# Feature projections on two 64-row array tiles, batch 1 loaded ahead of the MoE weights, and a planner that models shared DMA rings

## The chip, the cores and the metric

The kernel runs on one core of one Trainium2 chip. The metric is the device time of one execution in microseconds, as the median of several runs. A profile of one run gives the "span", the time from its first to its last instruction. The time is about 2 us longer than the span.

## The reference, cut to what matters

Two layers follow each other: a linear attention with random features (8 batches, 8 heads, 576 positions, 64 dimensions, 128 features), and an MLP ("MoE" in the code) on its output.

```
def phi(x):                      # x: q or k, scaled
    proj = einsum('bhsd,md->bhsm', x, omega)      # contraction over only d = 64
    h = proj - sum(x * x) / 2
    return exp(h - max(h)) / sqrt(m)
kv  = einsum('bhsm,bhsd->bhmd', phi(k), v);  z = sum_s phi(k)
out = einsum('bhsm,bhmd->bhsd', phi(q), kv) / (phi(q) . z + 1e-6)
x   = out as (4608, 512)
h   = x @ w_in                   # 512 -> 2048
y   = (h * sigmoid(1.702 h)) @ w_out              # 2048 -> 512
```

The two MLP products take 1152 matmuls of 512 columns. At the 0.216 us per matmul that the trace shows (0.86 us for four) that is 249 us, three quarters of the time.

## The kernel before

The program is planned when it is built. Every operation is put into a graph with an estimated cost and a priority, a small simulation decides the order on each engine, and the engines then run that order with semaphores.

Attention works in 32 steps: 8 batches of 4 head pairs. Q and K of a step lie transposed in a tile TT with 128 rows: 64 rows are the dimensions of one position, the other 64 those of its neighbour. Omega stands twice in a block-diagonal matrix omB, so that one matmul over 128 rows projects both positions; half of what it multiplies is zero.

```python
        for hd, t0, c0, o in (("a", 2, 0, 1280), ("b", 6, 4, 1792)):       # K: two banks
            gr = bank()
            g.add(PE,
                [mm(at(gr, 0, 256), Tb(t0), omB[:, :]), mm(at(gr, 256, 512), Tb(t0 + 1), omB[:, :])],
                240, key, reads=[("Tk", tt)] + OM, grp=gr)
            reduce(0, 4, c0, gr)                                            # DVE: max
            exp(gr, 512, o, ["k" + hd], key + 200)                          # ACT
        gr = bank()                                                         # tail: last 64 positions
        g.add(PE, [mm(at(gr, 128, 256), TLo, om_o), mm(at(gr, 0, 128), om_e, TLo)], 115, key + K_L, ...)
        ...
        for nm, w_, o in (("q0", om_e, 0), ("q1", om_o, 512)):              # Q: two banks
            gr = bank()
            g.add(PE, mm(at(gr, 0, 512), w_, Tq), 216, key + K_Q, ...)
            exp(gr, 512, o, [nm], key + K_Q + 100)
```

From batch 2 on, Q and K are transposed by DMA (into TT), and so is the attention's output (from OO into XT, the input of the MLP), all on the queue of SP. The heads of Q and K for the next batches are loaded by POOL's queue. At the start the loads go in this order: batch 0, half of batch 1's Q and K, w_in, the other half, w_out.

The softmax here doesn't subtract the row's maximum and nothing guards it: scores larger than these inputs give would overflow.

## Time and profile before

| | before |
|---|---|
| time, median | 329.97 us |
| span of the profiled run | 328.3 us, granted clock 0.995 |
| PE busy | 311.3 us, 95% |
| DVE, ACT, POOL busy | 58%, 60%, 26% |

These lines are from the page of the kernel before: the busy time of each engine, the busy share of PE and the granted clock in 40 slices of the span (9 is 90% or more), and the chain of work that ended last.

```profile
PE 311.3 (95%) x2091; PEld 163.2 (50%) x2129; DVE 189.5 (58%) x420; ACT 197.1 (60%) x396; POOL 86.6 (26%) x176
...
PE   2697999999999999999999999999999999999995
...
PEclk9989999999999999999999999999999999999999
...
PE 88%; DVE 5%; DMA 2%; issue 1%; SPq 1%; POOL 0%; ACT 0%; POOLq 0%
```

PE is busy 90% or more everywhere but in the first four slices and the last. A PE that is busy isn't yet at its peak, so the price of the projections is read from start to start. The next lines are PE's timeline of the kernel before in a late step (start in us, length in us, engine, line, operation, output and inputs, rows and columns, shape, count). A length contains about 0.16 us of pipeline that the next matmul overlaps. A few matmul records are missing from a trace, so a group of four can show as three.

```profile
233.33 0.22 PE L363 MATMUL PB<-omB,TL 128*128 128x128 bf16 x1
233.39 0.22 PE L363 MATMUL PB<-TL,omB 128*128 128x128 bf16 x1
233.44 0.38 PE L363 MATMUL PB<-TT,omB 128*128 128x512 bf16 x1
233.66 1.03 PE L363 MATMUL HT<-XT,WIN 128*128 128x512 bf16 x4
...
235.39 0.38 PE L363 MATMUL PB<-TT,omB 128*128 128x512 bf16 x1
235.60 1.03 PE L363 MATMUL HT<-XT,WIN 128*128 128x512 bf16 x4
...
237.64 0.60 PE L363 MATMUL PB<-omB,TT 128*128 128x256 bf16 x4
238.08 1.03 PE L363 MATMUL HT<-XT,WIN 128*128 128x512 bf16 x3
```

Tail 0.11 us (233.33 to 233.44), one half of Q 0.22 us, the other 0.21, K 0.44 us (237.64 to 238.08): 0.98 us per step.

The third view gives busy times by stretch for the kernel before; the columns are length, then busy us (count) of PE, PEld, DVE, ACT and POOL, then granted clock, DMA share and GB/s.

```profile
0.00:60.00 60.00, 48.72 (x432) 29.61 (x438) 39.33 (x102) 40.41 (x87) 30.83 (x60) 0.97 1.09 182
...
140.00:180.00 40.00, 39.69 (x289) 21.32 (x293) 26.86 (x64) 27.07 (x57) 14.89 (x30) 1.00 0.99 180
180.00:200.00 20.00, 19.89 (x131) 10.28 (x132) 13.40 (x28) 13.67 (x29) 3.04 (x8) 1.00 0.92 177
```

PE has some 11 us without work in the first 60 us and 0.1 to 0.2 us in each 20 us later.

### The profile page before, as it was taken

Reading aid. Unit: us, or ns where it says so; the run is one execution under the profiler, and the core shown is the slowest. Engines: PE = TensorE matmul, PEld = TensorE weight load, DVE = VectorE, ACT = ScalarE, POOL = GpSimd, SP = SyncE. Lnnn points to the kernel's source line nnn. Section 1 sums busy time; section 2 is a strip of 40 time slices with the busy share of each in tenths; the row PEclk is TensorE's granted clock in tenths of the full one; section 3 lists DMA queues with packets and bytes.
Section 4 is the critical chain, followed back from the end, with each engine's and each line's share of the span. In section 5 each row is a group of like instructions: output and inputs, shape, how many; then the busy total and the mean of one; then the engine's idle time right before and its main releaser. Section 6 shows DMA issues by size and latency. Waiting matters only on the chain.

```text
span 328.3 us, 5569 instructions
## 1 busy us (share of the span) xinstructions
PE 311.3 (95%) x2091; PEld 163.2 (50%) x2129; DVE 189.5 (58%) x420; ACT 197.1 (60%) x396; POOL 86.6 (26%) x176
## 2 busy tenths in 40 slices
PE   2697999999999999999999999999999999999995
PEld 1474655455555555555555555555544444444442
DVE  3397975458538786677468667675565434434300
ACT  2879664567738868777566657665663434344411
POOL 8398043043425226233316022222220000000000
PEclk9989999999999999999999999999999999999999
DMA  7999989989999999969979973311121011000033
GB/s 114 215 229 206 224 143 129 290 159 213 216 190 200 241 160 183 234 150 163 279 142 174 268 100 87 84 53 54 52 54 52 32 48 50 32 34 32 32 90 73
DMA packets 92939, 44.97 MB, mean 137 GB/s; under 512 B 59632, under 2 KB 88304, under 8 KB 92912
## 3 DMA queue, kind: packets, MB, share of 16 engines
q1 hardware_dynamic: 71760, 32.03, 44.3%
q0 software_dynamic: 21152, 12.59, 27.6%
q8 instruction: 17, 0.28, 0.4%
q14 instruction: 10, 0.08, 0.1%
HBM read 36.73 MB, written 9.44 MB: 141 GB/s over the span
## 4 chain that ended last, share of the span: by engine, by line
PE 88%; DVE 5%; DMA 2%; issue 1%; SPq 1%; POOL 0%; ACT 0%; POOLq 0%
PE OB L363 37%; PE HT L363 37%; PE PB L363 8%; PE SB L363 5%; DMA VS<-in_v_dram 2%; DVE NM L592 2%; DVE OO L733 1%; SPq L425 1%; DVE GT L792 1%; DVE TT L499 1%; PE SB L746 0%; SPq L447 0%; DVE RD L725 0%; POOL VP L652 0%; PE OB L534 0%
## 5 line engine op out<-in xcount | busy, mean ns | idle before, releaser
L792 DVE SCALAR_TENSOR_TENSOR GT<-TH,HT 128x512 bf16<-128x512 f32 x144 | 98.3, 685 | 75.6 <-ACT TH L787 75.1
L363 PE MATMUL HT<-XT,WIN 128*128 128x512 bf16 x555 | 139.6, 379 | 2.1 <-ACT WW L636 0.8
L363 PE MATMUL OB<-WOUT,GT 128*128 128x512 bf16 x559 | 137.8, 379 | 0.9
L787 ACT ACTIVATE TH<-HT 128x512 f32<-128x512 f32 x144 | 85.9, 597 | 73.8 <-PE HT L363 70.9
L603 ACT ACTIVATE QKP<-PB 128x512 bf16<-128x512 f32 (+1 forms) x143 | 77.8, 556 | 25.4 <-DVE NM L592 19.3
L363 PEld LDWEIGHTS OB<-WOUT,GT 128*128 128x128 bf16 x576 | 55.4, 98 | 59.9
L363 PEld LDWEIGHTS HT<-XT,WIN 128*128 128x128 bf16 x576 | 54.7, 98 | 58.4 <-ACT XT L498 0.9
L592 DVE TENSOR_REDUCE NM<-PB 128x4 f32<-128x512 f32 (+1 forms) x89 | 48.8, 564 | 26.1 <-PE PB L363 25.9
L641 POOL TENSOR_TENSOR WW<-WW,mask 128x2 f32<-128x2 f32 x32 | 6.3, 196 | 145.4 <-ACT WW L636 145.4
L652 POOL TENSOR_TENSOR VP<-VS,WW 128x512 bf16<-128x512 f32 x32 | 33.5, 1048 | 2.2 <-DMA VS<-in_v_dram 2.2
L821 ACT ACTIVATE OS<-OB 128x512 f32<-128x512 f32 x36 | 21.5, 597 | 20.6 <-PE OB L363 20.5
L733 DVE TENSOR_TENSOR OO<-SB,RD 128x320 bf16<-128x320 f32 x61 | 27.2, 478 | 0.1
L363 PE MATMUL PB<-omB,TT 128*128 128x256 bf16 x124 | 22.3, 282 | 1.7 <-ACT QKP L603 0.9
L363 PE MATMUL PB<-TT,omB 128*128 128x512 bf16 x54 | 19.7, 379 | 0.0
L363 PEld LDWEIGHTS SB<-KVZ,QKP 128*128 128x128 bf16 x305 | 14.0, 98 | 6.7 <-issue 0.2
L363 PEld LDWEIGHTS SB<-VP,QKP 128*128 128x128 bf16 x279 | 12.9, 99 | 8.1 <-POOL VP L662 2.3
L363 PE MATMUL SB<-VP,QKP 128*128 128x65 bf16 (+1 forms) x279 | 14.8, 198 | 2.0 <-POOL VP L662 1.8
L410 POOL DMA_DIRECT2D QK<-in_k_dram x17 | 13.4, 791 | 11.4 <-DMA TT<-QK 7.5
L363 PEld LDWEIGHTS PB<-omB,TT 128*128 128x128 bf16 x124 | 11.1, 100 | 8.6 <-ACT QKP L603 1.6
L363 PE MATMUL SB<-KVZ,QKP 128*128 128x65 bf16 x305 | 15.1, 195 | 0.0
L499 DVE CAST KVZ<-SB 128x130 bf16<-128x130 f32 x30 | 8.7, 289 | 11.0 <-PE SB L363 10.7
L410 POOL DMA_DIRECT2D QK<-in_q_dram x17 | 13.0, 766 | 0.0
(68 smaller groups left out, 134.0 us busy)
## 6 DMA issues: line engine op xcount, KB each, us to landing
out_dram<-OS SPq DMA_DIRECT2D x32, 256.0 KB, 2.5
VS<-in_v_dram SPq DMA_DIRECT2D x12, 512.0 KB, 8.8
QK<-in_k_dram POOLq DMA_DIRECT2D x15, 256.0 KB, 7.2
QK<-in_q_dram POOLq DMA_DIRECT2D x15, 256.0 KB, 8.9
VS<-in_v_dram SPq DMA_DIRECT2D x8, 256.0 KB, 8.4
WIN<-in_moe_w_in_dram POOLq DMA_DIRECT2D x4, 512.0 KB, 10.1
WOUT<-in_moe_w_out_dram POOLq DMA_DIRECT2D x4, 512.0 KB, 17.4
QLF<-in_q_dram SPq DMA_DIRECT2D x16, 64.0 KB, 4.4
```

Of the source, the lines that this page charges most:

```text
L363: return lambda e: e.matmul(o() if callable(o) else o, lhsT=l, rhs=r, **kw)
L410: POOL, lambda e, dst=dst, so=so: e.dma_start(dst, so), 800, key,
L425: SP, lambda e, dst=dst, so=so: e.dma_start(dst, so), 120, key,
L499: fv = lambda e: e.tensor_copy(out=o, in_=src())
L592: lambda e: e.tensor_reduce(out=NM[vs][:, c0 : c0 + w], in_=bass.AP(TILE[gr.bank], i, [[512, 128], [128, w], [1, 128]]), axis=AX.X, op=ALU ...
L603: lambda e: e.activation(out=X[:, o : o + w], in_=at(gr, 0, w)(), func=ACTF.Exp, scale=scale),
L641: lambda e: e.tensor_tensor(out=WW[vs][:, 0:2], in0=bass.AP(WW[vs], 10, [[12, 128], [0, 2]]), in1=mask2[:, :], op=ALU.mult,),
L652: lambda e: e.tensor_tensor(out=VP[vs][:, 2:10, 0:64], in0=bass.AP(V, vo + 64, [[vrow, 128], [64, 8], [1, 64]]), in1=bass.AP(WW[vs], 2, [[ ...
L733: lambda e, gr=gr, x=x: e.tensor_tensor(out=OO[os_][:, 5 * x : 5 * x + 5, :], in0=bass.AP(TILE[gr.bank], 0, [[512, 128], [65, 5], [1, 64]] ...
L787: lambda e, gr=gr, th=th: e.activation(out=TH[th][:, :], in_=at(gr, 0, 512)(), func=ACTF.Tanh, scale=0.851),
L792: lambda e, gr=gr, th=th, jc=jc: e.scalar_tensor_tensor(out=GT[gi][:, jc, :], in0=TH[th][:, :], scalar=1.0, in1=at(gr, 0, 512)(), op0=ALU. ...
L821: lambda e, gr=gr, os_=os_: e.activation(out=OS[os_][:, :], in_=at(gr, 0, 512)(), func=ACTF.Copy, scale=0.5),
```

## The change

The intent: a contraction over 64 rows needs only half of the array, so two such products can run side by side on two tiles of 64 rows. From batch 2 on, the K projections of even and odd positions run as pairs, and so do those of Q, K and Q in one visit of PE that fills four PSUM banks (JOIN). The tail is projected once per batch for all four steps. Batches 0 and 1 stay on full rows. Batch 1's Q and K are all loaded before w_in. V of batches 2 to 7 moves from SP's queue to POOL's (V_SW). The planner gets costs for the visits (PEC, in ns) and a model in which the DMA queues share the rings; all priorities were searched anew.

```diff
+PE_T = (0, 1)
+JOIN = True
+V_SW = 2
+PEC = dict(K=325.0, Q=315.0, KQ=540.0, L=345.0)
 ...
+        rt = b not in PE_T
+        lo = (slice(0, 64), slice(64, 128)) if rt else (slice(0, 128), slice(0, 128))
+        OMR = [omB[lo[par], 128 * par : 128 * par + 128] for par in range(2)]
+        def project(cols, cost, kk, reads):
+            gs = [bank() for _ in cols]
+            ems = [[mm(at(gr, o, o + w), l, r) for o, w, l, r in c] for gr, c in zip(gs, cols)]
+            if rt:
+                em = [f for j in range(0, len(ems), 2) for fs in zip_longest(*ems[j : j + 2]) for f in fs if f is not None]
+                g.add(PE, em, PEC[cost], kk, reads=reads + OM, grp=gs)
 ...
+        if rt and JOIN:
+            gr = project(kcols + qcols, "KQ", key, [("Tk", tt), ("Tq", tt)])
 ... (DMA queues in the planner: a queue's rate falls when the other is active)
-    load_qk(1, 0, 4, P["LD"] + -10, "a", after=[("k", 0, 0)])
-    for c in range(4):
-        load_win(c, P["LD"] + -5 + c, after=gate)
-    load_qk(1, 4, 4, P["LD"] + 0, "b", after=gate)
+    for c in range(4):
+        load_win(c, P["Lw"] + c, after=gate)               # Lw = 769
+    load_qk(1, 0, 4, P["Lb"], "a", after=gate)             # Lb = -19112: first
+    load_qk(1, 4, 4, P["Lb"] + 2, "b", after=gate)
```

## The prediction

> **What bounds the kernel.** By the table of the page PE is busy 311.3 us (95%) of a 328.3 us span; DVE 58%, ACT 60%, POOL 26%. The busy-by-stretch view shows PE full from 40 us on (39.68 of each 40 us) until the last matmul at 324 us; then one eviction and one store. The chain of waits is 88% PE. The exception is the start: PE was busy 3.7, 7.8, 7.85 and 9.5 us in the first four stretches of 10 us (11 us idle). There DMA is saturated (0.84 to 1.27 of 16 engines), and from 20 to 30 us DVE and ACT are busy 9.2 of 10 us. First MoE matmul: 29.9 us.
>
> **What the change saves.** In the PE timeline a steady attention step spends, start to start, 0.43 us on four 128x256 K projections, 0.43 on two 128x512 Q projections and 0.11 on the tail pair: 0.97 us. Half of the rows of each projection are zeros. From batch 2 on the change puts even and odd columns on two 64-row tiles side by side: half the columns, 0.43 us for K and Q together, and the tail once per batch. The Trainium skill, "TensorEngine Tiling (Array Packing)", Key Properties, says that tiles run in parallel but that changing the tiling mode drains the engine. This trace has no mode change; a matmul lasts 379 ns at a spacing of 216, so a drain can expose up to 0.16 us. The new planner's constants are 540 ns for the joint visit and 345 for the tail, about 110 ns over the half-length stream; I take these as estimates. Per step: 0.54 + 0.345/4 = 0.63 us instead of 0.97, saving 0.345; times 24 steps = 8.3 us, all on the critical path because PE is the limit there. With free switches it would be about 11 us; with 0.16 us in and out, about 4.
>
> Batches 0 and 1 stay on full rows: no change. POOL, DVE and ACT get slightly less work, off the path.
>
> **What it adds.** A joint visit opens all four P/S banks at once, so PE, in order, must find all four evacuated; a step has about 8 us and needs about 2.4 us of exps. I allow 1 us of new small PE waits. V loads of batches 2 to 7 move to POOL's queue: no cost expected.
>
> **The start.** W_in now comes behind all of batch 1's Q and K (1.2 MB newly ahead of it: about 5 us at that stretch's 220 GB/s). So the first MoE matmul moves to about 33 us, with batch 1's attention further along. ACT and DVE are nearly full there, so little PE work can be pulled forward; better planning should give back a bit. I book -2 us, doubt 3 us either way.
>
> **Sum.** 329.8 - 8.3 + 1 - 2 = 320.5; I shade to 319.5 us. Range 314 to 325. Faster by over 2% (below 323.2): 0.79; same: 0.19; slower: 0.02.
>
> **What would show it.** Projections per step near 0.55 us in the PE timeline from batch 2 on, pairs of 64-row matmuls starting within a few ns; PE still full (under 0.3 us idle per 20 us) from 40 us; a batch period of about 33.0 us instead of 34.3; first MoE matmul at 32 to 35 us; PE idle of the first 40 us within 3 us of the old 11.
>
> **What would make it wrong.** Drains of over 0.3 us per visit; tiles that don't overlap; PE waits for exps before joint visits; weights so late that PE starves between 30 and 60 us; loads of later batches late because PE now outruns the DMA (still 93% busy from 160 to 200 us).

## The result, and the profile after

| | before | after |
|---|---|---|
| time, median of 4 runs | 329.97 us (329.63 to 330.24) | 325.63 us (325.16 to 326.83) |
| ratio | | 0.9873, 95% interval 0.9851 to 0.9895 |
| span of the profiled run | 328.3 us | 323.0 us |
| PE busy | 311.3 us | 305.2 us |

A ratio is the mean time of one kernel's fast runs over that of the other's of the same rounds, so it isn't quite the ratio of the medians. The change gained 1.3%, not the 3.1% of the prediction, and the time lies 0.6 us above the stated range. From the page of the new kernel, busy times and chain:

```profile
PE 305.2 (94%) x2194; PEld 152.3 (47%) x2233; DVE 191.9 (59%) x394; ACT 194.2 (60%) x389; POOL 91.1 (28%) x149
...
PE 84%; DMA 9%; ACT 3%; POOL 2%; issue 1%; DVE 0%; POOLq 0%
```

DMA has 9% of the chain, where it had 2%. (The chain counts the whole length of a transfer that it passes through, not only the time that PE waited for it.) Next, PE's timeline of the new kernel around a tail visit, and then around a joint visit.

```profile
64.52 1.03 PE L412 MATMUL HT<-XT,WIN 128*128 128x512 bf16 x4
65.48 0.39 PE L412 MATMUL SB<-TL,omB 64*128 64x512 bf16 x1
65.48 0.39 PE L412 MATMUL PB<-omB,TL 64*128 64x128 bf16 x4
65.81 0.39 PE L412 MATMUL OB<-WOUT,GT 128*128 128x512 bf16 x1
```

```profile
66.68 1.03 PE L412 MATMUL HT<-XT,WIN 128*128 128x512 bf16 x4
67.64 0.23 PE L412 MATMUL SB<-omB,TT 64*128 64x128 bf16 x1
67.64 0.23 PE L412 MATMUL PB<-omB,TT 64*128 64x128 bf16 x1
...
67.82 0.22 PE L412 MATMUL SB<-omB,TT 64*128 64x128 bf16 x1
67.82 0.22 PE L412 MATMUL PB<-omB,TT 64*128 64x128 bf16 x1
67.87 0.38 PE L412 MATMUL SB<-TT,omB 64*128 64x512 bf16 x1
67.88 0.38 PE L412 MATMUL PB<-TT,omB 64*128 64x512 bf16 x1
68.18 1.04 PE L412 MATMUL OB<-WOUT,GT 128*128 128x512 bf16 x4
```

The tiles do work in parallel: the two matmuls of a pair start at the same hundredth of a microsecond or 0.01 us apart. But look at the edges. Four matmuls that start at 66.68 take 0.864 us of stream, so the next could have started at 67.54; it starts at 67.64. The last pair starts at 67.87 and streams 0.216 us, so the next could have come at 68.09; it comes at 68.18. Each change between 128-row and 64-row matmuls costs about 0.10 us. The joint visit takes 0.64 us (67.54 to 68.18), not 0.54; the tail visit 0.43 us (65.38 to 65.81), not 0.345. Over the visits of the trace, without those that have a matmul record missing at an edge, it is 0.64 and 0.43 us.

What fills these 0.10 us is seen in part in the weight loads (PEld) of the same visit:

```profile
67.63 0.09 PEld L412 LDWEIGHTS SB<-omB,TT 64*128 64x128 bf16 x1 [0.42 <-issue]
...
67.82 0.09 PEld L412 LDWEIGHTS SB<-TT,omB 64*128 64x128 bf16 x1
68.18 0.33 PEld L412 LDWEIGHTS OB<-WOUT,GT 128*128 128x128 bf16 x3 [0.26 <-issue]
```

Within a mode a weight load runs under the matmul before its own: the load at 67.82 is for the matmul at 67.87. The first load behind a change starts only with its own matmul (67.63 and 68.18), about 0.09 us after the last stream ended. These lines don't tell whether PE waits before that load or for it: both are part of the price of a change here.

By stretch, in the new kernel:

```profile
0.00:60.00 60.00, 50.19 (x466) 30.25 (x471) 40.44 (x95) 41.60 (x87) 31.52 (x53) 1.00 1.14 203
...
140.00:180.00 40.00, 39.47 (x294) 19.36 (x298) 28.05 (x59) 26.96 (x55) 11.87 (x19) 1.00 0.87 170
180.00:200.00 20.00, 18.53 (x155) 8.98 (x157) 10.34 (x24) 12.13 (x27) 9.51 (x15) 1.00 1.17 204
```

The start has improved, and from 180 to 200 us PE, which was idle for 0.1 us there, now is for 1.5. The wait table of the new kernel (who waited for whom: us, times, longest) has this line:

```profile
PE HT L412 <- DMA XT<-OO: 1.4, 1, 1.4
```

and the chain between 170 and 205 us (start, us, what) holds

```profile
187.24 10.68 DMA XT<-OO
```

This is the DMA that transposes the last part of batch 5's attention output. It landed 10.7 us after its issue; the median of these 24 transposes is 2.7 us. The timeline of POOL shows what had been issued shortly before, the loads of batch 7 (in brackets: idle time before, and what ended it):

```profile
180.03 0.80 POOL L459 DMA_DIRECT2D QK<-in_k_dram  x1 [5.22 <-DMA TT<-QK]
...
...
182.50 0.76 POOL L459 DMA_DIRECT2D QK<-in_q_dram  x1
183.23 1.54 POOL L506 DMA_DIRECT2D VS<-in_v_dram  x2
```

The books of the two profiled runs, from these readings:

| term | predicted | read from the traces |
|---|---|---|
| projections of batches 2 to 7 | -8.3 us | 24 x 0.98 = 23.5 before; 24 x 0.64 + 6 x 0.43 = 17.9 after: -5.6 us |
| new waits | +1 us | +1.4 us, one wait |
| start | -2 us | 7 more MLP matmuls issued by 60 us, both with batches 0 and 1 finished: 7 x 0.216 = -1.5 us |
| shading | -1 us | nothing stands behind it |
| sum | -10.3 us | -5.7 us; the spans differ by 5.3 |

The medians differ by only 4.3 us. The profiled run of before was one of its longer ones: it had a spell of clock 0.83 between 10 and 20 us, and other runs of it with clock 1.0 had spans of 327.2 to 328.8 us. The seven recorded runs of before with a mean clock of 0.992 to 0.995 have a mean span of 328.4 us, the other 35 have 327.9, so some 0.5 us of the start's 1.5 may belong to that spell. The times don't confirm the rest: projections and wait alone make -5.6 + 1.4 = -4.2 us, which is already the difference of the medians. The profiled pair shows an earlier start of 1.5 us; how much of it an undisturbed run gains is not shown, and it may be nothing.

### The profile page after: what moved, and what is told of

The parts are those of the page before. It is cut to its first block, busy times and chain, and to the rows that moved or that the text cites. A ratio compares the mean times of both kernels' runs of the same rounds, so it can differ in the third digit from the quotient of the medians.

```text
span 323.0 us, 5692 instructions
## 1 busy us (share of the span) xinstructions
PE 305.2 (94%) x2194; PEld 152.3 (47%) x2233; DVE 191.9 (59%) x394; ACT 194.2 (60%) x389; POOL 91.1 (28%) x149
## 4 chain that ended last, share of the span: by engine, by line
PE 84%; DMA 9%; ACT 3%; POOL 2%; issue 1%; DVE 0%; POOLq 0%
PE HT L412 38%; PE OB L412 31%; PE PB L412 8%; DMA QK<-in_q_dram 6%; PE SB L412 5%; DMA XT<-OO 3%; POOL QK L459 1%; ACT QKP L653 1%; ACT QKL L653 1%; ACT TH L854 0%; ACT OS L888 0%; PE PB L812 0%; PE PB L577 0%; DVE GT L859 0%; POOL ident L418 0%
## 5 line engine op out<-in xcount | busy, mean ns | idle before, releaser
L412 PE MATMUL OB<-WOUT,GT 128*128 128x512 bf16 x495 | 122.5, 379 | 1.4 <-issue 0.8
L653 ACT ACTIVATE QKP<-PB 128x512 bf16<-128x512 f32 x61 | 35.7, 605 | 3.2 <-PE SB L412 2.7
L653 ACT ACTIVATE QKP<-SB 128x512 bf16<-128x512 f32 x59 | 34.7, 602 | 4.0 <-PE PB L412 2.2
L643 DVE TENSOR_REDUCE NM<-PB 128x4 f32<-128x512 f32 x33 | 22.4, 685 | 9.8 <-PE SB L412 9.7
L643 DVE TENSOR_REDUCE NM<-SB 128x4 f32<-128x512 f32 x25 | 17.1, 688 | 11.9 <-PE PB L412 11.0
L799 DVE TENSOR_TENSOR OO<-SB,RD 128x320 bf16<-128x320 f32 x31 | 15.2, 491 | 1.0
L412 PE MATMUL PB<-WOUT,GT 128*128 128x512 bf16 x62 | 15.2, 379 | 0.1
L799 DVE TENSOR_TENSOR OO<-PB,RD 128x320 bf16<-128x320 f32 x27 | 13.3, 492 | 0.9
L412 PE MATMUL PB<-omB,TT 64*128 64x128 bf16 (+1 forms) x132 | 11.1, 220 | 0.2
L412 PE MATMUL SB<-TT,omB 64*128 64x512 bf16 (+1 forms) x34 | 10.8, 377 | 0.0
```

The source lines that it names most:

```text
L412: return lambda e: e.matmul(o() if callable(o) else o, lhsT=l, rhs=r, **kw)
L643: lambda e: e.tensor_reduce(out=o, in_=bass.AP(TILE[gr.bank], 0, [[512, 128], [128, 4], [1, 128]]), axis=AX.X, op=ALU.max, negate=True,),
L653: lambda e: e.activation(out=o, in_=at(gr, 0, 512)(), func=ACTF.Exp, scale=scale),
L799: lambda e, gr=gr, x=x: e.tensor_tensor(out=OO[os_][:, 5 * x : 5 * x + 5, :], in0=bass.AP(TILE[gr.bank], 0, [[512, 128], [65, 5], [1, 64]] ...
```

## The experiments

Theory A: the gain missing in the projections is the price of the mode changes, 0.10 us each, 60 of them, of which the planner's costs held only about half (0.11 us per visit). Rival B: they are nearly free, as the planner's costs have it, and the visits are long for another cause, such as slow 64-row matmuls or weight loads. Rival C: the tiles save nothing, and the gain is all start and order. A second theory, D, says that the wait near 197 us comes from batch 7's loads.

The first four experiments keep the planned order: only what PE does within a visit is changed, while the planner sees the old costs.

### e1_full_rows: the same visits on all 128 rows

```diff
-        lo = (slice(0, 64), slice(64, 128)) if rt else (slice(0, 128), slice(0, 128))
+        lo = (slice(0, 128), slice(0, 128))
```

> The new kernel with the same order on every engine, but the projections of batches 2 to 7 run on all 128 rows (zeros in half of them) instead of two 64-row tiles. Theory A (each change of the tiling mode costs PE about 0.10 us, 0.20 us per visit, read from the gaps around the visits): a joint visit goes from 0.64 to 0.86 us and a tail visit stays at 0.43 us, so +24 x 0.22 = +5.4 us against the new kernel, that is about 331 us. Rival B (mode changes are nearly free, as in the prediction): +24 x 0.32 + 6 x 0.1 = +8.3 us or more, about 334 us. Rival C (the tiles save nothing and the whole gain came from order and start): +0 us.

Measured: 329.69 us, ratio to before 0.9996 (0.9976 to 1.0015), which is 4.1 us above the new kernel's first median. Its order on every engine is the same as the new kernel's. PE's timeline of a joint visit in this run:

```profile
66.86 1.03 PE L412 MATMUL HT<-XT,WIN 128*128 128x512 bf16 x4
67.72 0.22 PE L412 MATMUL SB<-omB,TT 128*128 128x128 bf16 x1
...
68.17 0.38 PE L412 MATMUL SB<-TT,omB 128*128 128x512 bf16 x1
68.38 0.38 PE L412 MATMUL PB<-TT,omB 128*128 128x512 bf16 x1
68.60 0.59 PE L412 MATMUL OB<-WOUT,GT 128*128 128x512 bf16 x2
```

No gaps at the edges, 0.88 us (67.72 to 68.60) instead of 0.64. That makes 24 x 0.24 = 5.8 us, near A's 5.4; and its wait table has no wait of PE on the output transpose any more, which gives 1.4 back: 4.4 us expected from the two, 4.1 measured. B's 8.3 us and C's 0 are out. The experiment can't tell A from a visit that is long for another cause, since either way it has 0.64 us to lose; e2 and e3 are for that. Without the tiles the rest of the change is worth nothing that these runs can resolve.

### e2_extra_switch and e3_extra_mm: the mode change by itself

One useless 128-row matmul is added to each joint visit, in e2 between the K and the Q half, in e3 (the control) at its head. Its output is overwritten by the Q projection.

```diff
                 em = [... as before ...]
+                if cost == "KQ":
+                    em.insert(8, mm(at(gs[2], 0, 128), ident[:, :], ident[:, :]))     # e2
+                    em.insert(0, mm(at(gs[2], 0, 128), ident[:, :], ident[:, :]))     # e3 instead
```

> The new kernel with one extra, useless 128-row matmul of 128 columns between the K and the Q half of each joint visit (24 of them), so that each visit changes the mode four times instead of twice. Its result is overwritten. Theory A: +24 x (0.056 + 0.20) = +6.1 us against the new kernel, and +4.8 us against e3_extra_mm. Rival B (the visit is long because the 64-row matmuls and their weight loads are slow, not because of the mode changes): +24 x 0.056 = +1.3 us, as in e3.

> Control for e2_extra_switch: the same extra 128-row matmul at the head of each joint visit, next to other 128-row matmuls, so that no mode change is added. Both theories: +24 x 0.056 = +1.3 us against the new kernel, about 327 us.

Measured: e2 330.21 us, e3 326.66 us, on the same chip in the same rounds: 3.6 us apart for two more changes in each of 24 visits. In e3's trace PE still waited 0.7 us on the output transpose, and in e2's it didn't, so the changes themselves cost about 4.3 us, 0.09 us each. (e3 is 1.0 us above the new kernel's first median, where the stream of the 24 matmuls is 1.3.) PE's timeline in e2:

```profile
67.89 0.22 PE L412 MATMUL SB<-omB,TT 64*128 64x128 bf16 x1
67.90 0.22 PE L412 MATMUL PB<-omB,TT 64*128 64x128 bf16 x1
68.05 0.23 PE L412 MATMUL SB<-ident 128*128 128x128 bf16 x1
68.21 0.39 PE L412 MATMUL SB<-TT,omB 64*128 64x512 bf16 x1
68.21 0.39 PE L412 MATMUL PB<-TT,omB 64*128 64x512 bf16 x1
68.53 0.82 PE L412 MATMUL OB<-WOUT,GT 128*128 128x512 bf16 x3
```

A matmul of 128 columns streams 0.056 us. From 67.90 to 68.05 are 0.15 us, from 68.05 to 68.21 are 0.16: each time 0.10 us more than the stream. A holds as to the price: it comes with the change of mode, not with 64-row matmuls as such. B's e2 equal to e3 is out.

### e5_tail_full_rows: only the tail on full rows

```diff
-  [(0, 512, OMR[0], TLf[lo[0], :, :]...)], [(128 * i, 128, TLf[lo[1], i, :], OMR[1]) for i in range(NT)]
+  [(0, 512, OMF[0], TLf[:, :, :]...)],     [(128 * i, 128, TLf[:, i, :], OMF[1]) for i in range(NT)]   # OMF: all 128 rows; both lines shortened
```

> The new kernel with only the tail visit (once per batch, six visits) on 128 rows instead of two tiles, same order. Theory A: the halved stream of 0.22 us plus 0.20 us of mode changes equals the full stream of 0.43 us, so the tiles gain nothing there: 0 us, within 0.5 us. Rival B (mode changes nearly free): +6 x 0.1 to 0.2 = +0.6 to +1.3 us.

Measured: 325.17 us, ratio to before 0.9861 (0.9839 to 0.9882). The new kernel has 0.9873 and, in the last call, 0.9855. The intervals are about 0.7 us wide to each side, so the times alone don't put out B's +0.6. The trace does: the tail visit of e5 runs from 65.61 to 66.05 us, 0.44 us on full rows against 0.43 on tiles. The tiles gain nothing in the tail visit: half of 0.43 us is saved by streaming and paid for two mode changes.

### e4_no_join: K and Q in two visits

```diff
-JOIN = True
+JOIN = False
```

> The new kernel with K and Q in two separate visits per step (each on two tiles), planned anew with the same constants. Theory A (0.20 us of mode changes per visit): 24 visits more, +24 x 0.20 = +4.8 us of PE time against the new kernel, less about 1.4 us if PE then no longer waits for the transposed output of batch 5 near 196 us: +3.4 to +4.8 us, 329 to 330.5 us, no better than the kernel before. Rival B (mode changes nearly free): within 1 us of the new kernel.

Measured: 331.63 us, ratio 1.0054 (1.0028 to 1.008): 6.0 us above the new kernel and slower than the kernel before. The size was missed in both of its parts. The planner put some of the K and Q visits next to each other, so the trace has 42 separate stretches of 64-row work instead of 30: 12 x 0.20 = 2.4 us, not 4.8. And PE waited 3.5 us on output transposes and 1.2 on a Q/K transpose, 3.3 us more than in the new kernel. I expected the old wait to vanish; the new plan made others. The joining is needed: a half visit alone costs 0.22 + 0.20 = 0.42 us on tiles, against 0.43 on full rows.

### e6_late_loads7: batch 7 loaded later

```diff
             gate = [("wout", 2)] if b == 1 else [("tgo", b, 2)]
+            if b == 6:
+                gate = gate + [("xt", 3, 5)]
```

> The new kernel with the loads of batch 7 (Q, K, V) held until the last output transpose of batch 5 has landed; the order of PE changes a little near the end. Theory D (the 1.4 us that PE waited near 197 us is the transpose DMA of batch 5, 10.7 us from issue to landing, held up by the 3.5 MB of batch 7 issued 4 to 7 us before it): the transpose lands in under 5 us, the wait is gone, and the span is 0.7 to 1.4 us shorter, unless batch 7's own transposes now come late. Rival E (the transpose is slow for another cause): the wait stays and the time is unchanged.

Measured: 324.28 us, ratio 0.9832 (0.9809 to 0.9855). Both were run again side by side.

> The new kernel, unchanged, run beside e6_again on the same chip, because their first results came from different calls. About 325.6 us, PE waiting about 1.4 us for the transposed output of batch 5 near 197 us.

> The kernel of e6_late_loads7, unchanged, beside the new kernel in the same rounds. If holding back batch 7's loads is what saves the wait: 1.0 to 1.6 us below a_after_again. If the earlier difference came from the chip or the call: within 0.5 us of it.

Measured: 325.22 us (324.38 to 325.40) for the new kernel, ratio 0.9855 (0.9835 to 0.9875), and 323.64 us (323.46 to 323.83), ratio 0.9813 (0.9796 to 0.983), with the loads held back: 1.6 us less. In the new kernel PE waited 1.3 us on the transpose, as before. In the trace of e6_again no PE wait on a transpose is left. Its timelines have the issue of batch 5's last output transpose on SP, and its reader on PE at work without a wait:

```profile
186.34 1.21 SPq L822 DMA_TRANSPOSE XT<-OO  x1
...
190.53 1.90 PE L412 MATMUL HT<-XT,WIN 128*128 128x512 bf16 x8
```

By the trace it landed at 188.94 us, 2.6 us after its issue, where it took 10.7 us beside the loads; the output transpose before it took 2.7 us, where it had taken 7.1. In the same kernel's first profile, POOL issued the loads of batch 7 from 190.84 us. Theory D holds, with one reservation: the planner also changed the order on PE in the last third, so the experiment doesn't change the loads alone.

### e7_half_first: the old order of loads at the start

```diff
-    load_qk(1, 4, 4, P["Lb"] + 2, "b", after=gate)
+    load_qk(1, 4, 4, P["Lw"] + 10, "b", after=gate)
```

> The new kernel with the second half of batch 1's Q and K loaded after the input weights again, as the kernel before had it, planned anew with the same priorities (tuned for the other order, so the later stages may also lose a little). Theory F (the new order is worth about 1 us in the first 60 us, read from PE's progress in the two traces): PE has 1 to 3 us more idle time before 60 us than the new kernel. Rival G (the order is worth nothing; the start gained by other means): PE idle before 60 us within 0.5 us. Total time 326.5 to 331 us.

Measured: 335.23 us as the median of six runs, one of them slow; 334.57 for the five fast runs, which spread from 331.99 to 336.23; ratio 1.0135 (1.0095 to 1.0176). That is outside what either theory expected. Most of it isn't the start: PE waited 3.9 us on an output transpose near 136 us and had many small waits, in a plan whose priorities were tuned for the other order. In the first 60 us, 106 weight loads of MLP matmuls had started instead of 116, 2.2 us of work less, and PE was busy 47.6 us instead of 50.2, 2.6 us less. That lies in theory F's range, but stale priorities would show in the same way. The start's 1.5 us is read from one pair of traces; which part of the change made it stays open.

### c1_consts, v1_best, v2_best: can better planning get more?

The planner forecast a span of 317.8 us for the new kernel. If its visit costs are set to the measured ones, it forecasts 321.9, and the 1.4 us wait would make up the rest to 323.0 to 323.7. So it looks as if the forecast was wrong by about the mode changes that it had left out. But 321.9 belongs to the order that the planner then makes (c1), not to the new kernel's, so this is no more than rough.

```diff
-PEC = dict(K=325.0, Q=315.0, KQ=540.0, L=345.0)
+PEC = dict(K=425.0, Q=415.0, KQ=640.0, L=435.0)          # c1, v1 and v2
```

v1 and v2 also hold back the loads of batch 7, and their priorities come from a new search on the planner's forecast; for v1 the planner allowed 1.5 us more for each transpose during the search, for v2 it didn't.

> The new kernel with only the planner's costs of the projection visits corrected to what the traces show (joint visit 640 instead of 540 ns, tail 435 instead of 345), planned anew with the same priorities. With these costs the planner itself predicts a span of 321.9 us instead of 317.8; the new kernel's measured spans are 323.0 to 323.7. If the wrong constants only mis-sized the forecast: time within 1.5 us of the new kernel's 325.6 us. If they also led to a bad order (the wait for batch 5's transposed output): about 1.4 us less, 324.2 us.

> A version meant to beat both: corrected visit costs, the loads of batch 7 held back as in e6_late_loads7, 1.5 us more allowed for each transpose DMA, and the priorities searched again on the planner's forecast, which is 320.9 us of span. No PE wait on a transpose DMA after 40 us; span 320.5 to 322 us, time 322.5 to 324 us, so 0.3 to 1.8 us below e6_late_loads7.

> As v1_best, but with priorities searched without the extra allowance for transpose DMAs; the planner's forecast is 320.7 us of span. Same time as v1_best within 0.5 us if the forecast of the transposes is good enough; slower by over 1 us, with a PE wait on a transpose DMA, if not.

| | forecast span | measured spans | time | ratio to before |
|---|---|---|---|---|
| c1_consts | 321.9 | 324.5 to 325.0 | 326.73 us | 0.9913 (0.9897 to 0.9928) |
| v1_best | 320.9 | 323.2 to 324.3 | 325.78 us | 0.9879 (0.9861 to 0.9897) |
| v2_best | 320.7 | 331.6 to 335.5 | 334.60 us | 1.0144 (1.0121 to 1.0168) |

None of the three was better than the new kernel, and the corrected costs alone were worse by over 1 us. c1 and v1 lie 2.3 to 3.4 us over their forecasts; in v1 PE waited for no output transpose, so that what its forecast misses stays open. For v2 the wait table shows where the forecast breaks:

```profile
PE HT L407 <- DMA XT<-OO: 10.1, 2, 5.5
```

Two output transposes landed 9.3 and 13.0 us after issue; the planner's largest figure for one in that plan was 8.8. So the search had picked an order that the model was too kind to; that a search tends to do so is my reading, not shown. The version that beats both kernels is therefore the new one with batch 7's loads held back.

## Why the prediction was wrong

- **What bounds the kernel, and that the projections lie on the critical path: right.** PE stayed full outside the start; e1 turns 5.8 us of PE stream into 4.1 us of time, the rest being, within the noise, a wait that it removes.
- **"about 110 ns over the half-length stream": this step failed.** The projections saved 5.6 us, not 8.3. The term that was mis-sized is the cost of a visit: 0.64 and 0.43 us measured, where the prediction had 0.54 and 0.345. The two mode changes of a visit cost 0.20 us together, as the gaps and e2 against e3 show, and there are 30 visits. The prediction had a bracket of its own from the trace, 4 to 11 us depending on the change's price, and then took the planner's constants as if they had been measured.
- **"I allow 1 us of new small PE waits": the size was nearly right, the cause wrong.** There was one wait of 1.4 us, and it wasn't for exps before a joint visit but for a transpose DMA beside the loads of a later batch. "Loads of later batches late because PE now outruns the DMA", in the list of what could go wrong, came near it: PE was held up by late output, and e1's slower PE didn't wait, though the same transpose took 9.6 us there. The slow landing itself isn't new: in the kernel before, the longest took 10.0 us, and PE waited for none.
- **"V loads of batches 2 to 7 move to POOL's queue: no cost expected": not tested by itself.** These loads are part of the 3.5 MB beside which the transpose was slow.
- **The start: -2 us booked, 1.5 read from the profiled pair, and hardly any of it confirmed by the times.** The first MLP matmul came at 30.4 us, not at 33; with the old order of loads in e7 it came at 26.9, so the direction of the delay was right.
- **"I shade to 319.5 us": failed.** The prediction gives no reason for it, and the constants were optimistic, not cautious. Without the shading, the result would still have been far from 320.5.
- **"Pairs of 64-row matmuls starting within a few ns": right** (0 to 10 ns). "PE still full (under 0.3 us idle per 20 us)" failed from 180 to 200 us, where PE lacked 1.5 us of work.

The Trainium skill, "TensorEngine Tiling (Array Packing)", Key Properties, names the drain at a mode change; the trace agrees in that each change has a gap, and gives it a size, 0.10 us. That the array drains in it is not seen in these views. "TensorE: Matmul & The Clock Gate", Part 3, has tiles starting within about 4 ns; at the resolution of these lines the trace agrees. "DMA: Bandwidth & Descriptors", Queues, rings and completion order, says that each DMA engine serves its queues in turn; I infer that a transfer on SP's queue can be slowed by POOL's. The 10.7 us against a median of 2.7 and e6's missing wait are in keeping with that; no run here shows the turns themselves.

## What to carry to other kernels

In these runs two row tiles pay only when the halved stream saves more than the two mode changes of 0.10 us each. A visit must have more than about 0.4 us of full-row stream to gain at all, so put all 64-row work that can be had into one visit; here K with Q gained 0.24 us, and K, Q or the tail alone next to nothing (0.42 to 0.43 us on tiles against 0.43 to 0.44). Before a gain is booked, look for a cost that the old trace can't contain, give it its bracket, and measure it with a small pair of kernels that differ only in that cost. And when PE becomes faster, look at what it catches up with: a transfer that used to be early may have to share the rings with the next batch's loads.

## What the Trainium skill lacked or had wrong

- "TensorEngine Tiling (Array Packing)", Key Properties, says that a mode change drains TensorE, but gives no price. Here it is about 0.10 us in each direction between 128-row and 64-row matmuls of bf16 (gaps at 67.54 to 67.64 and 68.09 to 68.18 us; e2 against e3). Its table of speedups ("Up to 2×") has no word on how long a visit must be; a visit with 0.43 us of full-row stream gained nothing on tiles (e5) and one with 0.88 us gained 0.24.
- "TensorE: Matmul & The Clock Gate", Back-to-back issue gap, gives about 131 ns per 512-column and 81 ns per 128-column matmul as the sustained spacing of a stream with weight loads. The traces show, at a granted clock of 1.00, 216 ns (four in 0.864 us) and 56 ns (eight in 0.45 us in e1), each matmul with its own weight load. These are the values that the page has for the isolated gap.
- "DMA: Bandwidth & Descriptors" has no duration of a transpose between places in SBUF beside other traffic. Here, in the new kernel and its variants, a 128 x 640 bf16 transpose took 2.6 to 2.8 us from issue to landing in the median, and 7.6 to 13.0 us as the longest of a run; in the new kernel the longest was beside the loads of a batch, and took 2.6 us when these were held back.
